# Transposing K on VectorE as 4-byte pairs, with scores in 32-row tiles and no row maximum, in a one-core attention kernel

## The chip, the cores and the metric

The kernel runs on one core of a Trainium2 chip. The metric is the device time of one execution in microseconds (us); less is better. Engines are called as in the profile: PE is TensorE (PEld its weight loads), DVE is VectorE, ACT is ScalarE, POOL is GpSimd, SP is SyncE, which issues the loads.

## The reference

Two independent attention blocks, A and B, run on their own inputs and their outputs are concatenated. Each block is:

```python
# x [16,64,640]  k_cache, v_cache [16,32,512,128]  wq [640,4096]  wo [4096,640], all bf16
q = (x @ wq).reshape(16, 64, 32, 128).transpose(0, 2, 1, 3)
scores = einsum("bhqd,bhkd->bhqk", q, k_cache) * 128 ** -0.5
p = softmax(scores, axis=-1)
o = einsum("bhqk,bhkd->bhqd", p, v_cache)
return o.transpose(0, 2, 1, 3).reshape(16, 64, 4096) @ wo
```

The caches are 16 x 32 x 512 x 128 x 2 bytes = 67 MB each, four of them, so about 268 MB of the 295 MB that are read are K and V. One property of the data matters for the experiments: x, K and wq are scaled so that a score has a standard deviation near 0.001. The softmax is therefore almost uniform, and the comparison with the reference cannot see keys that are taken in a wrong order. Where an experiment has a wrong key order on purpose, this is said, and its passing the comparison means nothing. For the same reason, where a version that moves the permutation is called right below, its key order rests on the indices of its access patterns, which lead to V's order; the comparison alone could not show it.

## The kernel before

The unit of work is two heads of two batches (a batch has 64 queries, so two batches fill 128 rows). Four engines run fixed orders of such units, shifted against each other like a pipeline; SP loads ahead into rings of buffers. For one unit PE transposes K (KX, 2 x 8 matmuls against the identity), DVE copies the result out of PSUM (KE), PE projects the queries (QP2), scores them (SM2), DVE takes row maxima (MX), ACT takes the exponential with the row sum (EX), DVE the reciprocal (RC2), POOL normalises (NM), PE transposes P (TR2), DVE copies it (TE2), then PE does PV and the output projection.

```python
PE_T = (("TR2", 1), ("QP2", 4), ("KX", 4, 0), ("SM2", 3), ("PV2", 1), ("XT", 0), ("OP2", 0), ("KX", 4, 1))
DVE_T = (("TE2", 1), ("RC2", 2), ("KE", 4, 0), ("MX", 3, 0), ("MX", 3, 1), ("KE", 4, 1), ("OVF", 0))
POOL_T = (("NM", 0, 0), ("NM", 0, 1))
# ... (cut)
def em_KX(e, op):                                    # PE: K to PSUM, transposed
    for t8 in range(8):
        ins = e.transpose(kt_ps[:, t8, :], kn_ring[:, c % NKB, j, hp, t8, :], ident[:, :])
def em_KE(e, op):                                    # DVE: PSUM to SBUF
    ins = e.tensor_copy(dst, src)                    # 128 x 1024 bf16
def em_SM2(e, op):                                   # PE: 4 matmuls, 128 rows x 64 columns
    ins = e.matmul(s_bank(sub)[64 * j:64 * j + 64, :], qT_ring[:, m % NQ, sub, 64 * j:64 * j + 64],
                   ktp_ring[:, m % NKT, sub, j, :], start=True, stop=True, tile_position=(0, 64 * j))
def em_MX(e, op):
    ins = e.reduce_max(negmax[:, r:r + 1], s_bank(g % 2), axis=AX.X, negate=True)
def em_EX(e, op):
    ins = e.activation(p_ring[:, g % NP, :], s_bank(g % 2), ACTF.Exp, bias=negmax[:, r:r + 1], scale=1.0,
                       accum_out=rowsum[:, r:r + 1])
def em_NM(e, op):                                    # POOL: normalise, and put keys in V's order
    src = p_ring[:, g % NP, :].rearrange("q (th tl pp) -> q th tl pp", th=2, tl=4)
    dst = pn_ring[:, g % NPN, :].rearrange("q (tl pp th) -> q th tl pp", tl=4, th=2)
    ins = e.tensor_scalar(dst, src, recip[:, r:r + 1], 1.0, ALU.mult, ALU.mult)
# ... (cut)
```

K and V are loaded in different key orders, so something has to permute the columns of P, and here POOL does it while it normalises. With `th=2`, consecutive elements of a run of `pp` are written two bf16 elements apart: a step of 4 bytes.

Of the kernel before, what the change touches and what calls it, by code (L numbers as in the profile page):

```python
# [6 lines left out]
F32 = mybir.dt.float32  # L7
ACTF = mybir.ActivationFunctionType
# [3 lines left out]
ENGINES = ("sp", "pe", "act", "dve", "pool")  # L12


class Cfg:
    G = 4
    HH = 16
    NKB = 5
    NVB = 5
    NX = 2  # L20
    NXN = 1
    XLEAD = 10
    NQ = 2
    NKT = 2
    NP = 4
    NPN = 3
    NT = 2
    NO = 2
    NR = 8
    PE_T = (("TR2", 1), ("QP2", 4), ("KX", 4, 0), ("SM2", 3), ("PV2", 1), ("XT", 0), ("OP2", 0), ("KX", 4, 1))  # L30
    ACT_T = (("QE2", 4), ("OE2", 1), ("XE", 0), ("EX", 3, 0), ("EX", 3, 1), ("OV", 0), ("ST", -1))
    DVE_T = (("TE2", 1), ("RC2", 2), ("KE", 4, 0), ("MX", 3, 0), ("MX", 3, 1), ("KE", 4, 1), ("OVF", 0))
    POOL_T = (("NM", 0, 0), ("NM", 0, 1))
    TAIL_SPLIT = 2
    SLOT_NS = 3600.0
    DMA_NS = dict(LDK=3100.0, LDV=3100.0, LDWQ=3900.0, LDWO=4300.0, LDX=700.0)


class Op:
    __slots__ = ("eng", "kind", "idx", "reads", "writes", "sem", "count", "deps", "waits", "dur", "ts", "aux",  # L40
                 "dma")

    def __init__(self, eng, kind, idx, reads=(), writes=(), dur=0.0, ts=None, aux=None):
        self.eng = eng
        self.kind = kind
        self.idx = idx
        self.reads = tuple(reads)
        self.writes = tuple(writes)
        self.sem = None
        self.count = None  # L50
        self.deps = []
        self.waits = []
        self.dur = dur
        self.ts = ts
        self.aux = aux
        self.dma = kind in ("LDK", "LDV", "LDX", "LDWQ", "LDWO", "ST")


STAGES = ("LDW", "LDX", "LDK", "LDV", "KX0", "KE0", "KX1", "KE1", "QP2", "QE2", "SM2", "MX0", "MX1", "EX0", "EX1",
          "RC2", "NM0", "NM1", "TR2", "TE2", "XT", "XE", "PV2", "OE2", "OP2", "OV", "ST")  # L60
STAGE_IDX = {s: i for i, s in enumerate(STAGES)}
SUB_KINDS = ("KX", "KE", "EX", "NM", "MX")


def build_plan(dims, cfg):
    NBLK, B, H = dims["NBLK"], dims["B"], dims["H"]
    G = cfg.G
    HH = min(cfg.HH, H)
    assert H % HH == 0 and HH % G == 0 and G % 2 == 0 and cfg.NR % 2 == 0 and B % 2 == 0
    NHALF = H // HH  # L70
    assert NHALF in (1, 2)
    NBP = B // 2
    SPB = HH
    NPASS = NBLK * NHALF
    NSTEP = NPASS * NBP * SPB
    NMAC = NSTEP // 2
    NCHUNK = NSTEP // G
    NGRP = NPASS * NBP
    HG = HH // G
    MPG = SPB // 2  # L80
    MPP = NBP * MPG
    MPC = G // 2
    KT = dims["KT"]

    def step_info(g):
        grp = g // SPB
        return grp // NBP, grp % NBP, grp, g % SPB

    progs = {e: [] for e in ENGINES}

    def mk(eng, kind, idx, reads, writes, stage, m_ts, sub=0, aux=None, dur=0.0):
        return Op(eng, kind, idx, reads, writes, dur=dur, aux=aux, ts=(m_ts, STAGE_IDX[stage], sub))

    OFF = {}
    for t in cfg.PE_T:
        OFF.setdefault(t[0], t[1])

    def make_op(kind, m, sub):
        g0, g1 = 2 * m, 2 * m + 1
        ps_, bp, grp, h0 = step_info(g0)  # L100
        c = g0 // G
        if kind == "KX":
            return mk("pe", "KX", (m, sub), [("kn", c % cfg.NKB, g0 % G), ("kn", c % cfg.NKB, g1 % G), ("ident",)],
                      [("KTB",)], "KX%d" % sub, m, sub)
        if kind == "KE":
            return mk("dve", "KE", (m, sub), [], [("KTB",), ("ktp", m % cfg.NKT, sub)], "KE%d" % sub, m, sub)
        if kind in ("MX", "EX", "NM"):
            g = 2 * m + sub
            r = g % cfg.NR
            if kind == "MX":  # L110
                return mk("dve", "MX", g, [], [("SB", sub), ("negmax", r)], "MX%d" % sub, m, sub)
            if kind == "EX":
                return mk("act", "EX", g, [("negmax", r)], [("SB", sub), ("p", g % cfg.NP), ("rowsum", r)],
                          "EX%d" % sub, m, sub)
            return mk("pool", "NM", g, [("p", g % cfg.NP), ("recip", r)], [("pn", g % cfg.NPN)], "NM%d" % sub, m, sub)
        r0, r1 = g0 % cfg.NR, g1 % cfg.NR
        if kind in ("XT", "XE"):
            mt = m + cfg.XLEAD
            if mt % MPG != 0 or not (0 <= mt < NMAC):
                return None  # L120
            gq = mt // MPG
            m_ts = mt - cfg.XLEAD + OFF["TR2"]
            if kind == "XT":
                return mk("pe", "XT", gq, [("xn", gq % cfg.NXN), ("ident",)], [("PTB",)], "XT", m_ts, aux=gq)
            return mk("act", "XE", gq, [], [("PTB",), ("xT", gq % cfg.NX)], "XE", m_ts, aux=gq)
        if kind == "QP2":
            return mk("pe", "QP2", m, [("xT", grp % cfg.NX), ("wq", ps_ % 2, h0 // G)], [("QB",)], "QP2", m)
        if kind == "QE2":
            return mk("act", "QE2", m, [], [("QB",), ("qT", m % cfg.NQ)], "QE2", m)
        if kind == "SM2":  # L130
            return mk("pe", "SM2", m, [("qT", m % cfg.NQ), ("ktp", m % cfg.NKT, 0), ("ktp", m % cfg.NKT, 1)],
                      [("SB", 0), ("SB", 1)], "SM2", m)
        if kind == "RC2":
            return mk("dve", "RC2", m, [("rowsum", r0), ("rowsum", r1)], [("recip", r0), ("recip", r1)], "RC2", m)
        if kind == "TR2":
            return mk("pe", "TR2", m, [("pn", g0 % cfg.NPN), ("pn", g1 % cfg.NPN), ("ident",)], [("PTB",)], "TR2", m)
        if kind == "TE2":
            return mk("dve", "TE2", m, [], [("PTB",), ("pT", m % cfg.NT)], "TE2", m)
        if kind == "PV2":
            return mk("pe", "PV2", m, [("pT", m % cfg.NT), ("v", c % cfg.NVB, g0 % G), ("v", c % cfg.NVB, g1 % G)],  # L140
                      [("OB",)], "PV2", m)
        if kind == "OE2":
            return mk("act", "OE2", m, [], [("OB",), ("oT", m % cfg.NO)], "OE2", m)
        if kind == "OP2":
            return mk("pe", "OP2", m, [("oT", m % cfg.NO), ("wo", ps_ % 2, h0 // G)], [("OUTB",)], "OP2", m)
        if kind in ("OV", "OVF", "ST"):
            if h0 + 1 != SPB - 1:
                return None
            last_half = ps_ % NHALF == NHALF - 1
            if kind == "OV":  # L150
                if NHALF == 1:
                    return mk("act", "OV", m, [], [("OUTB",), ("out_sb", grp % 2)], "OV", m, aux=grp)
                if last_half:
                    return None
                return mk("act", "OVP", m, [], [("OUTB",), ("outp", bp)], "OV", m, aux=grp)
            if kind == "OVF":
                if NHALF == 1 or not last_half:
                    return None
                return mk("dve", "OVF", m, [("outp", bp)], [("OUTB",), ("out_sb", grp % 2)], "OV", m, aux=grp)
            if NHALF == 1 or not last_half:  # L160
                return None
            return mk("act", "ST", m, [("out_sb", grp % 2)], [("out_dram", grp)], "ST", m, aux=grp)
        raise ValueError(kind)

    templates = {"pe": cfg.PE_T, "dve": cfg.DVE_T, "pool": cfg.POOL_T, "act": cfg.ACT_T}
    for eng, tmpl in templates.items():
        offs = [t[1] for t in tmpl] + [cfg.XLEAD]
        for k in range(-max(offs), NMAC - min(offs)):
            for t in tmpl:
                kind, off = t[0], t[1]  # L170
                sub = t[2] if len(t) > 2 else 0
                if kind in ("XT", "XE"):
                    op = make_op(kind, k, 0)
                    if op is not None:
                        progs[eng].append(op)
                    continue
                m = k + off
                if 0 <= m < NMAC:
                    op = make_op(kind, m, sub)
                    if op is not None:  # L180
# [7 lines left out]

    loads = []
    NEG = -10 ** 9  # L190
    for ps_ in range(NPASS):
        first_m = ps_ * MPP
        buf = ps_ % 2
        for j in range(HG):
# [68 lines left out]
    for eng in ENGINES:  # L263
        for op in progs[eng]:
            if not op.dma:
                assign(op)
# [453 lines left out]
```

## Time and profile before

| | before |
|---|---|
| median of 3 runs | 958.7 us (958.1 to 958.71) |
| busy share: PE / DVE / ACT / POOL | 96% / 88% / 59% / 44% |
| mean of one normalisation, K eviction, maximum, exponential | 843, 691, 681, 684 ns |
| read from HBM | 294.65 MB |

From the page of the kernel before: the busy time of each engine, then the span in 40 equal slices (a digit is the busy share in tenths; the last line is what the DMA engines moved in each slice).

```profile
PE 919.4 (96%) x14755; PEld 733.5 (77%) x15008; DVE 841.9 (88%) x1552; ACT 567.1 (59%) x1585; POOL 416.9 (44%) x518
...
PE   4999999999999999999999999999999999999997
...
POOL 0444444444444444444444444444444444444443
...
DMA  9999999999999999888999999988888988899830
GB/s 315 364 365 364 351 365 367 365 368 351 338 337 337 343 330 315 299 292 305 322 332 352 326 353 327 306 294 296 302 305 288 308 301 297 295 297 314 295 124 15
```

PE is full from the second slice on, at a granted clock of 0.998 on average. DMA moves about 365 GB/s while it fills the rings, and later follows PE, at 290 to 350.

From the same page, the chain of work that ended last (share of the span by engine), and four of its groups (line, engine, operation, output<-inputs, count | busy us, mean ns of one | idle before, and what ended it).

```profile
PE 89%; DVE 4%; POOL 3%; issue 2%; SPq 1%; DMA 1%; POOLq 0%; DVEq 0%
...
L496 POOL TENSOR_SCALAR pn_ring<-p_ring,recip 128x512 bf16<-128x512 bf16 x512 | 416.3, 843 | 532.7 <-DVE recip L488 532.7
L442 DVE COPY ktp_ring<-ps 128x1024 bf16<-128x1024 bf16 x512 | 353.7, 691 | 105.3 <-PE ps L433 85.1
L482 ACT ACTIVATE p_ring<-ps,negmax 128x512 bf16<-128x512 f32 x512 | 345.6, 684 | 4.8 <-DVE negmax L476 4.8
L476 DVE TENSOR_REDUCE negmax<-ps 128x1 f32<-128x512 f32 x512 | 327.3, 681 | 0.4 <-PE ps L467 0.3
```

So PE sets the pace. POOL's 843 ns per normalisation cost nothing here: it is idle for 532.7 us.

### The profile page before, as it was taken

What the parts mean: (1) busy time and instruction counts of PE and PEld (TensorE: products, weight loads), DVE (VectorE), ACT (ScalarE), POOL (GpSimd) and SP (SyncE); (2) the same over time, 40 slices, a digit from 0 to 9 for tenths busy, and PEclk for the clock granted to TensorE, in tenths of its full rate; (3) what the DMA queues carried; (4) which work ended last, traced back from release to release, by engine and by line L of the source; (5) the groups of instructions that cost most, each with busy time, mean ns of one, the idle gap of its engine ahead of it and who ended that gap; (6) DMA issues with size and microseconds to landing.
All of it is one profiled execution on the core that took longest, in us unless ns stands there. A gap on an engine that the chain in (4) does not pass through costs nothing.

```text
span 956.8 us, 34351 instructions
## 1 busy us (share of the span) xinstructions
PE 919.4 (96%) x14755; PEld 733.5 (77%) x15008; DVE 841.9 (88%) x1552; ACT 567.1 (59%) x1585; POOL 416.9 (44%) x518
## 2 busy tenths in 40 slices
PE   4999999999999999999999999999999999999997
PEld 3877777778777777877777787777877778777775
DVE  2898899898899999899999899889899998999996
ACT  1666656666665565656566666666666656565654
POOL 0444444444444444444444444444444444444443
PEclk9999999999999999999999999999999999999999
DMA  9999999999999999888999999988888988899830
GB/s 315 364 365 364 351 365 367 365 368 351 338 337 337 343 330 315 299 292 305 322 332 352 326 353 327 306 294 296 302 305 288 308 301 297 295 297 314 295 124 15
DMA packets 230871, 299.51 MB, mean 313 GB/s; under 512 B 9536, under 2 KB 165184, under 8 KB 230720
## 3 DMA queue, kind: packets, MB, share of 16 engines
q1 hardware_dynamic: 228416, 294.69, 91.0%
q8 instruction: 118, 1.93, 0.8%
q10 hardware_dynamic: 2304, 2.62, 0.8%
q14 instruction: 33, 0.27, 0.1%
HBM read 294.65 MB, written 2.62 MB: 311 GB/s over the span
## 4 chain that ended last, share of the span: by engine, by line
PE 89%; DVE 4%; POOL 3%; issue 2%; SPq 1%; DMA 1%; POOLq 0%; DVEq 0%
PE ps L433 22%; PE ps L524 14%; PE ps L451 14%; PE ps L467 14%; PE ps L505 12%; PE ps L545 7%; PE ps L540 5%; POOL pn_ring L496 3%; DVE out_sb L560 1%; DVE ktp_ring L442 1%; DVE pT_ring L512 1%; PE ps L604 1%; DMA xn_ring<-in_A_x_dram 1%; SPq L626 1%; SPq L583 1%
## 5 line engine op out<-in xcount | busy, mean ns | idle before, releaser
L496 POOL TENSOR_SCALAR pn_ring<-p_ring,recip 128x512 bf16<-128x512 bf16 x512 | 416.3, 843 | 532.7 <-DVE recip L488 532.7
L442 DVE COPY ktp_ring<-ps 128x1024 bf16<-128x1024 bf16 x512 | 353.7, 691 | 105.3 <-PE ps L433 85.1
L482 ACT ACTIVATE p_ring<-ps,negmax 128x512 bf16<-128x512 f32 x512 | 345.6, 684 | 4.8 <-DVE negmax L476 4.8
L476 DVE TENSOR_REDUCE negmax<-ps 128x1 f32<-128x512 f32 x512 | 327.3, 681 | 0.4 <-PE ps L467 0.3
L433 PE MATMUL ps<-ident,kn_ring 128*128 128x128 bf16 x4096 | 314.6, 220 | 2.8 <-DMA kn_ring<-in_A_k_cache_dram 1.6
L532 ACT ACTIVATE oT_ring<-ps 128x256 bf16<-128x256 f32 x256 | 98.0, 383 | 306.0 <-PE ps L524 306.0
L433 PEld LDWEIGHTS ps<-ident,kn_ring 128*128 128x128 bf16 x4096 | 251.9, 98 | 34.2 <-DVE ktp_ring L442 2.6
L524 PEld LDWEIGHTS ps<-pT_ring,v_ring 128*128 128x128 bf16 x4096 | 133.5, 98 | 109.2 <-issue 100.0
L451 PE MATMUL ps<-xT_ring,wq_sb 128*128 128x128 bf16 x2560 | 186.4, 220 | 3.2 <-DMA wq_sb<-in_A_wq_dram 3.2
L512 DVE COPY pT_ring<-ps 128x1024 bf16<-128x1024 bf16 x256 | 174.5, 682 | 4.6 <-PE ps L505 3.8
L524 PE MATMUL ps<-pT_ring,v_ring 128*128 128x64 bf16 x4096 | 163.8, 194 | 3.3 <-issue 1.7
L467 PE MATMUL ps<-ktp_ring,qT_ring 128*64 128x512 bf16 x1024 | 159.8, 392 | 0.4 <-ACT p_ring L482 0.4
L505 PE MATMUL ps<-ident,pn_ring 128*128 128x128 bf16 x2048 | 156.7, 219 | 3.5 <-POOL pn_ring L496 3.5
L451 PEld LDWEIGHTS ps<-xT_ring,wq_sb 128*128 128x128 bf16 x2560 | 155.2, 98 | 3.5 <-DMA wq_sb<-in_A_wq_dram 3.5
L459 ACT ACTIVATE qT_ring<-ps 128x256 bf16<-128x256 f32 x256 | 98.4, 384 | 66.8 <-PE ps L451 66.8
L505 PEld LDWEIGHTS ps<-ident,pn_ring 128*128 128x128 bf16 x2048 | 124.1, 98 | 7.0 <-POOL pn_ring L496 6.7
L545 PE MATMUL ps<-wo_sb,oT_ring 128*128 128x128 bf16 x512 | 112.1, 219 | 13.4
L482 ACT ACTIVATION_READ_ACCUMULATOR p_ring<-ps,negmax 128x1 f32 x512 | 105.0, 205 | 0.0
L540 PE MATMUL ps<-wo_sb,oT_ring 128*128 128x512 bf16 x259 | 97.8, 379 | 0.0
L540 PEld LDWEIGHTS ps<-wo_sb,oT_ring 128*128 128x128 bf16 x512 | 50.1, 98 | 30.6 <-ACT oT_ring L532 0.3
L467 PEld LDWEIGHTS ps<-ktp_ring,qT_ring 128*64 128x64 bf16 x1024 | 36.1, 108 | 27.1 <-ACT p_ring L482 0.6
L545 PEld LDWEIGHTS ps<-wo_sb,oT_ring 128*128 128x128 bf16 x512 | 50.1, 98 | 0.0
(13 smaller groups left out, 112.7 us busy)
## 6 DMA issues: line engine op xcount, KB each, us to landing
kn_ring<-in_A_k_cache_dram SPq DMA_DIRECT2D x128, 512.0 KB, 7.0
v_ring<-in_A_v_cache_dram SPq DMA_DIRECT2D x128, 512.0 KB, 7.2
kn_ring<-in_B_k_cache_dram SPq DMA_DIRECT2D x126, 512.0 KB, 4.8
v_ring<-in_B_v_cache_dram SPq DMA_DIRECT2D x126, 512.0 KB, 5.7
wq_sb<-in_A_wq_dram SPq DMA_DIRECT2D x8, 640.0 KB, 10.4
wo_sb<-in_A_wo_dram SPq DMA_DIRECT2D x8, 640.0 KB, 10.2
wq_sb<-in_B_wq_dram SPq DMA_DIRECT2D x8, 640.0 KB, 8.4
wo_sb<-in_B_wo_dram SPq DMA_DIRECT2D x8, 640.0 KB, 7.5
```

The source lines that it names most:

```text
L433: ins = e.transpose(kt_ps[:, t8, :], kn_ring[:, c % NKB, j, hp, t8, :], ident[:, :])
L442: ins = e.tensor_copy(dst, src)
L451: ins = e.matmul(q_ps[:, sub * 128:(sub + 1) * 128], wq_sb[:, ps_ % 2, kt, hh * DH:(hh + 1) * DH], xT_ring[:, grp % NX, kt, :], start=(kt ...
L467: ins = e.matmul(s_bank(sub)[64 * j:64 * j + 64, :], qT_ring[:, m % NQ, sub, 64 * j:64 * j + 64], ktp_ring[:, m % NKT, sub, j, :], start=T ...
L476: ins = e.reduce_max(negmax[:, r:r + 1], s_bank(g % 2), axis=AX.X, negate=True)
L482: ins = e.activation(p_ring[:, g % NP, :], s_bank(g % 2), ACTF.Exp, bias=negmax[:, r:r + 1], scale=1.0, accum_out=rowsum[:, r:r + 1])
L496: ins = e.tensor_scalar(dst, src, recip[:, r:r + 1], 1.0, ALU.mult, ALU.mult)
L505: ins = e.transpose(pt_ps[:, sub, t, :], pn_ring[:, g % NPN, t * 128:(t + 1) * 128], ident[:, :])
L512: ins = e.tensor_copy(pT_ring[:, m % NT].rearrange("p s t q -> p (s t q)"), pt_ps_flat)
L524: ins = e.matmul(o_ps[:, col:col + 64], v_ring[:, c % NVB, j, gi, t, :], pT_ring[:, m % NT, sub, t, 64 * j:64 * j + 64], start=(t == 0), s ...
L540: ins = e.matmul(out_ps0, oT_ring[:, m % NO, sub, :], wo_sb[:, ps_ % 2, hh, 0:N0], start=(hh == 0), stop=(hh == SPB - 1))
L545: last = e.matmul(out_ps1, oT_ring[:, m % NO, sub, :], wo_sb[:, ps_ % 2, hh, N0:DN], start=(hh == 0), stop=(hh == SPB - 1))
```

## The change

The intent is to take K's transposes off PE, the engine that is full. K is loaded with 16 keys per partition (4 KB rows instead of 2 KB). DVE transposes it with bf16 pairs taken as one 4-byte element, in blocks of 32x32 as the kernel's indices take them, which leaves the head dimension in a permuted order over 32 partitions. The columns of wq are permuted to match (POOL, once per chunk of four heads and block), and scores are summed over four rounds of eight 32-row tiles. The unit becomes a *pack* of four heads of two batches; there are 128 packs. The row maximum goes; at the end the row sums are checked, and if one lies outside 2^-40 to 2^40 a general second program with the maximum runs. Every operation gets its place in each engine's order from a table of times `AT`, in units of a pack.

```diff
-    PE_T = (("TR2", 1), ("QP2", 4), ("KX", 4, 0), ("SM2", 3), ...
-    DVE_T = (("TE2", 1), ("RC2", 2), ("KE", 4, 0), ("MX", 3, 0), ...
+    AT = dict(XT=-2 + 0.90, XE=-2 + 0.93, QP=-1 + 0.40, QE=-1 + 0.58, KT=(-1 + 0.08, -1 + 0.70), S=0.0,
+              EX=(0.20, 0.35, 0.55, 0.80), RC=(0.52, 0.93), NM=(0.54, 0.68, 0.95, 1.10),
+              TR=(0.95, 1.28), TE=(1.02, 1.38), PV=(1.20, 1.60), OE=(1.50, 1.72), OP=(1.70, 1.86),
+              OV=1.88, ST=1.885, WP0=-1.75, WP1=-6.0)
 ... (cut)
+    pending = sorted(loads, key=lambda e: (e[0], e[2]))
+    t_now = -8.0                                       # SP's order of loads is planned from here
 ... (cut)
-        def em_KX / em_KE                              # PE transposes, DVE evictions (cut)
+        def em_LDK(e, op):
+            src = blocks[blk][1][2 * bp + b, 4 * j:4 * j + 4].rearrange("h (p t) d -> (h p) (t d)", t=16)
+        def em_WP(e, op):                              # POOL: permute a chunk of wq, two copies (cut)
+        def em_KT(e, op):
+            dst = kt_ring[:, n % NKT, b].rearrange("p t j k two -> p (t j k two)").bitcast(F32)
+            ins = e.transpose(dst, kn_ring[:, n % NK, b, :].bitcast(F32))
+        def em_S(e, op):
+            for f in range(4):
+                for b in range(2):
+                    for i in range(4):
+                        rows = slice(32 * i, 32 * i + 32)
+                        last = e.matmul(ps[64 * b:64 * b + 64, i, :], qs_ring[rows, n % NQ, f, b, :],
+                                        kt_ring[rows, n % NKT, b, :, f // 2, :, f % 2],
+                                        start=(f == 0), stop=(f == 3), tile_position=(32 * i, 64 * b))
-            ins = e.activation(p_ring[...], s_bank(g % 2), ACTF.Exp, bias=negmax[:, r:r + 1], ...
+            ins = e.activation(p_ring[:, h % NP, :], ps[:, h % 4, :], ACTF.Exp, scale=1.0, ...
         def em_NM(e, op):
-            src = p_ring[:, g % NP, :].rearrange("q (th tl pp) -> q th tl pp", th=2, tl=4)
-            dst = pn_ring[:, g % NPN, :].rearrange("q (tl pp th) -> q th tl pp", tl=4, th=2)
+            src = p_ring[:, h % NP, :].rearrange("q (th tl k) -> q th tl k", th=4, tl=4)
+            dst = pn_ring[:, h % NPN, :].rearrange("q (tl k th) -> q th tl k", tl=4, th=4)
```

The last two lines follow from the new load. K now has 16 keys per partition while V still has 4, so the permutation has `th=4`: the normalisation writes runs of 32 elements with a step of 8 bytes instead of runs of 64 with a step of 4.

## The prediction

> **What bounds it now.** TensorE. The busy table has PE at 919 of 957 us, DVE 88%, ACT 59%, POOL 44%; the granted clock is full; 89% of the chain that ended last is PE. In the timeline one unit (two heads, two batches) is 3.56 us of PE work: K transposes 2x0.45, query projection 0.56, scores 0.55 plus 0.18 of switching, P transposes 0.45, PV 0.45, output 0.52. A pack of four heads is two units, 7.13 us; 128 packs are 913 us. DMA is second: in slices 1 to 9 its share is 0.9 or more at 365 GB/s, until the rings are full; later it follows at about 300 GB/s.
>
> **Per pack, what changes** (durations from the trace).
> - PE: the 32 K transposes go, -1.8 us. Scores become 32 matmuls in four rounds of eight 32x64 tiles. [...] this trace has two column tiles starting 4 ns apart and 240 ns per round of N=512. Four rounds plus two switches of 0.09 us: about 1.15 us, as now. PE: about 5.3 us.
> - DVE: K evictions (4x0.69) and maxima (4x0.64) go, 5.3 us. Added: two 128x1024 four-byte transposes and a 128x512 query eviction (0.66). No trace shows a DVE transpose[...]. DVE: 4.7 us instead of 6.9.
> - ACT loses the query evictions: 3.3 us. POOL keeps 4x0.84 = 3.4 us; in 16 packs it also permutes wq, about 4 us (estimate from 1.65 ns an element).
> - Order of work: reciprocal, two normalisations (1.63), P transposes (0.45), projection (1.12), its eviction (0.62), K transpose (1.15), next reciprocal, with latencies: about 5.5 us a pack. PE's own loop is also about 5.5.
>
> **DMA takes over.** Counting packets in 2 us slices of the saturated stretch, a 1 KB packet costs an engine 47 ns (347 GB/s over 16 engines), 1280 B 56 ns, 2 KB 86-87 ns. Extrapolated (estimate), the new 4 KB K packets cost about 165 ns, 397 GB/s. K then needs 338 us, V (unchanged, 1 KB) 386, wq 30, wo 29, x 7 (read once, not twice), out 7, instruction fetch about 8: **805 us**; 5.65 us per pack without weights. That is just above the 5.5 us of compute, so I expect DMA saturated nearly throughout: 805 + 2 to start + 9 from the last V to output and flag check + a few us of stalls at the block change, where POOL's permutation makes packs last 8 us.
>
> **Prediction: 822 us** (14% less); 8 in 10 between 797 and 862. Faster by over 2%: 0.97; within 2%: 0.02; slower: 0.01.
>
> **What would show the steps.** DMA share above 0.95 and 355-375 GB/s in nearly all slices; waits on landed loads (K for the DVE transpose, V for PV) instead of an unbroken PE chain; DVE transpose 1.15-1.25 us; a pack's score matmuls in 1.0-1.2 us; no general rerun.
>
> **What would make it wrong.** [...] Reading the score operand at a stride of 4 bytes, or wq at 8 bytes, slowing PE: up to 6.2 us a pack, 850 us. In-order waits that add up (one set of score banks, one PV bank): 6 us a pack, 830-850. The 4 KB packets at V's rate per byte: 850[...].

What is cut above, and marked, rested on no trace or run of this case. For PE, the cut sentence held that a round's eight tiles run beside each other; the trace of the kernel before shows this for two column tiles alone, 3 to 4 ns apart, so that PE's 5.3 us and the scores' 1.15 rest on an estimate of mine. For DVE, the cut sentence held the duration of one transpose, again an estimate of mine that no trace showed. "DVE: 4.7 us" came to that with about 2.4 us for the two transposes, and "K transpose (1.15)" in the order of work and the range 1.15 to 1.25 us further down are the same estimate.

## The result

| | before | after |
|---|---|---|
| median (lowest to highest) | 958.71 us (958.1 to 958.84), 4 runs | 948.87 us (948.03 to 952.19), 4 runs |
| ratio after / before, 95% interval | | 0.9903 (0.9885 to 0.9921): within 2% |
| busy share: PE / DVE / ACT / POOL | 96 / 88 / 59 / 44% | 78 / 61 / 44 / 74% |

A ratio here and below is the mean time of one kernel's runs over the mean of the other's of the same rounds on the same chip, so it is not quite the ratio of the medians that stand beside it.

The prediction was 822 us, 797 to 862. The kernel takes 127 us more than that. The work did leave PE (178 us of busy time) and DVE (264 us), and the time hardly moved: the question is where the gain went. From the page of the kernel after, the same lines as of before:

```profile
PE 741.5 (78%) x13905; PEld 524.2 (55%) x13905; DVE 577.9 (61%) x902; ACT 418.6 (44%) x1313; POOL 700.1 (74%) x550
...
PE   3077888888888888887677888888888888888884
...
POOL 2099777777777778788777878787878777777774
...
DMA  9999999989999998997579999999999999999820
GB/s 332 366 368 342 367 325 307 336 305 330 318 327 312 318 331 307 324 362 271 199 236 377 373 375 378 376 372 327 327 315 319 325 311 332 305 334 317 300 86 12
```

No engine is full. DMA is above 370 GB/s only in the stretch after the block change, where it refills rings; between the filling of the rings and the change, and again later, it follows something at 300 to 340. Its busy digits hide this, because they are 9 there too: from 100 to 400 us the share is 0.93 to 0.96 at 320 to 329 GB/s, while from 20 to 35 us, where the rings fill, it is 1.06 at 370 GB/s (records of packets overlap, so the share can pass 1). The rate tells more than the digit. Two steps of the prediction already fail here: DMA was to be saturated nearly throughout, and POOL, which was to stay near 3.4 us a pack, has 700.1 us instead of 416.9. The chain and the groups of the same page say more:

```profile
POOL 72%; DVE 11%; PE 10%; SPq 4%; issue 2%; DMA 1%; ACT 0%; ACTq 0%
POOL pn_ring L436 68%; DVE pT_ring L449 9%; PE ps L444 8%; POOL wqp_sb L357 2%; POOL wqp_sb L356 1%; SPq L349 1%; SPq L335 1%; DVE recip L429 1%; PE ps L380 1%; DMA ws_ring<-in_A_wq_dram 1%; SPq L342 1%; DVE kt_ring L393 1%; DVE qs_ring L386 0%; PE ps L403 0%; PE ps L460 0%
...
L436 POOL TENSOR_SCALAR pn_ring<-p_ring,recip 128x512 bf16<-128x512 bf16 x512 | 662.9, 1417 | 195.9 <-DVE recip L429 195.9
L416 ACT ACTIVATE p_ring<-ps 128x512 bf16<-128x512 f32 x512 | 304.0, 596 | 358.7 <-PE ps L403 358.7
...
L393 DVE STREAM_TRANSPOSE kt_ring<-kn_ring 128x1024 f32<-128x1024 f32 x256 | 315.9, 1234 | 7.5 <-DMA kn_ring<-in_A_k_cache_dram 7.5
```

The normalisation has the same shape and type as before, and takes 1417 ns instead of 843. It is 68% of the chain. POOL is not full all the same: it idles 195.9 us, waiting for reciprocals. The timeline shows how a normalisation that leaves POOL idle can nevertheless set the pace. This is one pack in the steady stretch of the kernel after (start us, duration us, engine, line, operation, [idle before <- what ended it]; rows of other work left out):

```profile
297.97 1.42 POOL L436 TENSOR_SCALAR pn_ring<-p_ring,recip 128x512 bf16<-128x512 bf16 x1
...
299.44 0.62 PE L444 MATMUL ps<-ident,pn_ring 128*128 128x128 bf16 x8 [0.25 <-POOL pn_ring L436]
...
299.77 0.20 ACT L416 ACTIVATION_READ_ACCUMULATOR p_ring<-ps 128x1 f32 x1
...
300.10 0.69 DVE L449 COPY pT_ring<-ps 128x1024 bf16<-128x1024 bf16 x1 [0.66 <-PE ps L444]
...
300.71 0.16 DVE L429 RECIPROCAL recip<-rowsum 128x2 f32<-128x2 f32 x1
300.96 5.17 POOL L436 TENSOR_SCALAR pn_ring<-p_ring,recip 128x512 bf16<-128x512 bf16 x4 [1.57 <-DVE recip L429]
...
302.98 0.12 DVE L429 RECIPROCAL recip<-rowsum 128x2 f32<-128x2 f32 x1
303.67 0.62 PE L444 MATMUL ps<-ident,pn_ring 128*128 128x128 bf16 x8 [0.83 <-POOL pn_ring L436]
```

Follow it down. The last normalisation of a pack ends at 299.39; only then can PE transpose that P (299.44); DVE evicts it (300.10); and the next pack's first reciprocal stands *behind* that eviction in DVE's order (300.71), although the second of its two row sums was there at 299.97 (the ACT row); only then can POOL start the next four normalisations (300.96). The second reciprocal comes at 302.98, in time, so the four run back to back in 5.17 us. A pack is 5.17 + 1.57 = 6.74 us, and measured from first reciprocal to first reciprocal, nearly every pack from the seventh on, outside the block change, is 6.72 to 6.75. The records of neighbouring normalisations overlap a little: four of 1.42 take 5.17.

The span adds up from such periods. The first reciprocal is at 15.5 us; 127 intervals at 6.73 are 855; the first eight intervals are 36 longer than that (the first alone 33, see the experiment on the head); the eight at the block change (9.11 to 10.13 each) are 23 longer; from the last pack's first reciprocal to the end are 16. Together 946, the span. A DMA-bound pack would need 5.65 by the prediction.

### The profile page after: what moved, and what is told of

It is laid out like the page before. It is cut to its first block, busy times and chain, and to the rows that moved or that the text cites. A ratio compares the mean times of both kernels' runs of the same rounds, so it can differ in the third digit from the quotient of the medians. Undisturbed runs are those within 1.5% of the kernel's fastest.

```text
span 946.3 us, 31604 instructions
## 1 busy us (share of the span) xinstructions
PE 741.5 (78%) x13905; PEld 524.2 (55%) x13905; DVE 577.9 (61%) x902; ACT 418.6 (44%) x1313; POOL 700.1 (74%) x550
## 4 chain that ended last, share of the span: by engine, by line
POOL 72%; DVE 11%; PE 10%; SPq 4%; issue 2%; DMA 1%; ACT 0%; ACTq 0%
POOL pn_ring L436 68%; DVE pT_ring L449 9%; PE ps L444 8%; POOL wqp_sb L357 2%; POOL wqp_sb L356 1%; SPq L349 1%; SPq L335 1%; DVE recip L429 1%; PE ps L380 1%; DMA ws_ring<-in_A_wq_dram 1%; SPq L342 1%; DVE kt_ring L393 1%; DVE qs_ring L386 0%; PE ps L403 0%; PE ps L460 0%
## 5 line engine op out<-in xcount | busy, mean ns | idle before, releaser
L436 POOL TENSOR_SCALAR pn_ring<-p_ring,recip 128x512 bf16<-128x512 bf16 x512 | 662.9, 1417 | 195.9 <-DVE recip L429 195.9
L416 ACT ACTIVATE p_ring<-ps 128x512 bf16<-128x512 f32 x512 | 304.0, 596 | 358.7 <-PE ps L403 358.7
L393 DVE STREAM_TRANSPOSE kt_ring<-kn_ring 128x1024 f32<-128x1024 f32 x256 | 315.9, 1234 | 7.5 <-DMA kn_ring<-in_A_k_cache_dram 7.5
L444 PE MATMUL ps<-ident,pn_ring 128*128 128x128 bf16 x2048 | 159.9, 221 | 184.6 <-POOL pn_ring L436 184.6
L380 PE MATMUL ps<-xT_ring,wqp_sb 128*128 128x128 bf16 x2560 | 170.9, 224 | 2.1 <-POOL wqp_sb L357 1.3
L474 PE MATMUL ps<-wo_sb,oT_ring 128*128 128x512 bf16 x512 | 167.6, 385 | 0.0
L380 PEld LDWEIGHTS ps<-xT_ring,wqp_sb 128*128 128x128 bf16 x2560 | 156.8, 115 | 3.3 <-ACT p_ring L416 1.7
L403 PE MATMUL ps<-kt_ring,qs_ring 32*64 32x512 bf16 x4096 | 146.9, 398 | 1.9 <-DVE kt_ring L393 1.9
L386 DVE TENSOR_SCALAR qs_ring<-ps 128x512 bf16<-128x512 f32 x128 | 88.5, 692 | 52.6 <-PE ps L380 52.6
L416 ACT ACTIVATION_READ_ACCUMULATOR p_ring<-ps 128x1 f32 x512 | 105.4, 206 | 0.0
L403 PEld LDWEIGHTS ps<-kt_ring,qs_ring 32*64 32x64 bf16 x4096 | 55.5, 104 | 41.6 <-DVE kt_ring L393 2.2
```

Of the source, the lines that this page charges most:

```text
L380: last = e.matmul(ps[:, 0, f * 128:(f + 1) * 128], w[:, kt, f, :], xT_ring[:, xs, kt, :], start=(kt == 0), stop=(kt == KT - 1))
L386: ins = e.tensor_scalar(qs_ring[:, op.idx % NQ].rearrange("p f b q -> p (f b q)"), ps[:, 0, :], scale, None, ALU.mult)
L393: ins = e.transpose(dst, kn_ring[:, n % NK, b, :].bitcast(F32))
L403: last = e.matmul(ps[64 * b:64 * b + 64, i, :], qs_ring[rows, n % NQ, f, b, :], kt_ring[rows, n % NKT, b, :, f // 2, :, f % 2], start=(f = ...
L416: ins = e.activation(p_ring[:, h % NP, :], ps[:, h % 4, :], ACTF.Exp, scale=1.0, accum_out=rowsum[:, h:h + 1])
L436: ins = e.tensor_scalar(dst, src, recip[:, (h // 2) % NR, h % 2:h % 2 + 1], 1.0, ALU.mult, ALU.mult)
```

## The experiments

The theory: the 8-byte destination step makes the normalisation 1.7 times as long, and this length, through the hand-over above (the 1.57 us between a pack's last normalisation and the next pack's first), sets the pace; with the step back at 4 bytes, DMA takes over as predicted. The rivals: POOL is slowed by the DVE transposes that now run beside it; it is the shorter runs (32 instead of 64), not the step; or the time went to the start and the block change. The last two experiments keep the long normalisation and ask which order of work sets the 6.73 us of a pack.

### e1_step4B: the destination step alone, back at 4 bytes

```diff
-            src = ... "q (th tl k) -> q th tl k", th=4, tl=4      dst = ... "q (tl k th) -> q th tl k", tl=4, th=4
+            src = ... "q (th tl pp) -> q th tl pp", th=2, tl=4    dst = ... "q (tl pp th) -> q th tl pp", tl=4, th=2
```

The key order is wrong: everything else is the kernel after.

> Only the normalisation's destination changes: step 4 bytes in runs of 64, as the kernel before has it (wrong values on purpose, the same amount of work). Theory (the 8-byte step of POOL's writes makes the normalisation slow): 1417 ns falls to about 843 ns, the steady pack from 6.73 us to 5.65-5.8 us (DMA or the rest of the chain), the time to about 825 us (119 steady packs times 1.0 us less; the start and the block change keep most of their loss). Rival A (POOL is slowed by VectorE's new SBUF-to-SBUF transposes): the normalisation stays above 1.3 us and the time at 949. Rival B (in-order waits other than POOL set the pack): the normalisation falls to 0.84 us but the pack stays above 6.3 us, time above 900.

Measured: 828.5 us (826.16 to 831.45), ratio to before 0.8643 (0.8617 to 0.867). Its page, the normalisation and the DMA lines, and POOL's timeline in the same stretch:

```profile
DMA  9999999999999999999989999999999999999980
GB/s 329 364 372 369 378 377 376 378 374 377 374 375 376 361 378 377 379 371 371 330 285 376 375 377 377 374 376 376 380 369 377 376 374 378 375 373 375 378 286 13
...
L436 POOL TENSOR_SCALAR pn_ring<-p_ring,recip 128x512 bf16<-128x512 bf16 x512 | 418.3, 846 | 317.8 <-DVE recip L429 317.8
```

```profile
298.61 1.62 POOL L436 TENSOR_SCALAR pn_ring<-p_ring,recip 128x512 bf16<-128x512 bf16 x2 [1.57 <-DVE recip L429]
300.85 1.65 POOL L436 TENSOR_SCALAR pn_ring<-p_ring,recip 128x512 bf16<-128x512 bf16 x2 [0.62 <-DVE recip L429]
```

One access pattern is worth 120 us. The normalisation is back at 846 ns, DMA is saturated in nearly all slices, and outside the start and the block change nearly all packs are 5.45 to 6.9 us, about 5.9 on average, as loads allow. The hand-over of 1.57 us is still there; but with it POOL's round is about 4.8 us (3.27 + 1.57), shorter than the 5.45 that PE needs, so it no longer sets anything.

### e5_step4B_run32: step 4 bytes, runs of 32

```diff
-            src = ... "q (th tl k) -> q th tl k"            dst = ... "q (tl k th) -> q th tl k"
+            src = ... "q (two a k) -> q two a k", k=32      dst = ... "q (a k two) -> q two a k", k=32
```

Wrong key order; runs are as short as in the kernel after.

> The normalisation writes runs of 32 elements, as the kernel after does, but at a 4-byte step (wrong values on purpose). Theory (the step decides, not the length of the runs): 0.83-0.87 us each, time about 828 us. Rival (short runs cost POOL a restart each): above 1.1 us.

Measured: one run, 829.25 us, state unknown; the normalisation takes 844 ns in its profile. So it is the step, not the length of the runs; this rests on the duration in one profile.

### e3_before_8B: the kernel before with the 8-byte step

```diff
-            src = ... th=2, tl=4        dst = ... "q (tl pp th) -> q th tl pp", tl=4, th=2
+            src = ... th=4, tl=4        dst = ... "q (tl k th) -> q th tl k", tl=4, th=4
```

There is no DVE transpose in this kernel, and the step is all that it has of the change. Wrong key order.

> The kernel before with the kernel after's 8-byte step in the normalisation (wrong values on purpose); no DVE transpose in it. Theory: the normalisation goes from 843 to about 1417 ns although nothing else changed; POOL has 3.56 us per unit for 2.83, so the time stays within 2% (958-980). Rival A: the normalisation stays at 0.84 us, time 958.

Measured: 1118.34 us (1118.08 to 1118.86), ratio 1.1666 (1.1646 to 1.1685). Its chain and its normalisation:

```profile
POOL 57%; DVE 18%; PE 18%; issue 4%; SPq 1%; DMA 1%; POOLq 0%; DVEq 0%
...
L496 POOL TENSOR_SCALAR pn_ring<-p_ring,recip 128x512 bf16<-128x512 bf16 x512 | 679.7, 1411 | 427.3 <-DVE recip L488 427.3
```

The normalisation takes 1411 ns without any DVE transpose: contention with the transposes is refuted as its cause. The size of the result was a surprise: the expectation was a kernel that stays near PE's pace, since POOL's work of 2 x 1.33 us fits in a unit of 3.56. It does not fit in the *loop*, as a line of POOL's timeline in this run shows:

```profile
306.18 2.65 POOL L496 TENSOR_SCALAR pn_ring<-p_ring,recip 128x512 bf16<-128x512 bf16 x2 [1.57 <-DVE recip L488]
```

Two normalisations take 2.65, then P is transposed and evicted, and the next reciprocal stands behind that eviction in DVE's order: again 1.57 us of hand-over. A unit takes 2.65 + 1.57 = 4.22 us, with POOL 61% busy. The kernel before has the same hand-over in its order, and hides it only because its normalisations are short.

### e2_exp_permutes: the permutation moved to ACT

```diff
-            ins = e.activation(p_ring[:, h % NP, :], ps[:, h % 4, :], ACTF.Exp, ...
+            dst = p_ring[:, h % NP, :].rearrange("q (tl k th) -> q th tl k", tl=4, th=4)
+            ins = e.activation(dst, <ps, h % 4, as "q th tl k">, ACTF.Exp, ...
     em_NM: src and dst contiguous
```

The result is right.

> Right result: ScalarE's exp writes the permuted order (8-byte step), POOL's normalisation is contiguous on both sides. Theory: the normalisation takes at most 843 ns; if ScalarE does not mind the step, exp stays at 0.60 us, pack 5.65-5.8 us, time about 825 us. If ScalarE minds it as POOL does, exp goes to about 1.0 us, ScalarE to about 5 us a pack and the chain scores-exp-projection grows by 0.4-1.6 us: 6-7 us a pack, 860-950 us. Rival A: the normalisation stays above 1.3 us.

Measured: 925.1 us (923.0 to 926.64), ratio 0.9645 (0.9625 to 0.9666). The exponential with the 8-byte step and the contiguous normalisation:

```profile
ACT 56%; PE 33%; POOL 4%; SPq 4%; issue 2%; DMA 1%; DVE 0%; ACTq 0%
...
L418 ACT ACTIVATE p_ring<-ps 128x512 bf16<-128x512 f32 x512 | 660.0, 1343 | 185.3 <-PE ps L403 185.3
L439 POOL TENSOR_SCALAR pn_ring<-p_ring,recip 128x512 bf16<-128x512 bf16 x512 | 349.3, 696 | 481.4 <-DVE recip L432 481.3
```

ACT pays the same way: 1343 ns against 596 contiguous. The chain moves from POOL to ACT and a pack takes 6.62 us. The step's cost is no peculiarity of POOL.

### e7_kt_8B: half of the permutation in DVE's transpose

The DVE transpose writes 4-byte elements. Let it write one bit of the key order with a step of 8 bytes; the normalisation keeps the other bit, a step of 4 bytes. The result is right.

```diff
-        kt_ring = sb("kt_ring", [128, NKT, 2, 16, 2, 32, 2], BF16)
+        kt_ring = sb("kt_ring", [128, NKT, 2, 8, 2, 32, 2, 2], BF16)
-            ins = e.transpose(dst, kn_ring[:, n % NK, b, :].bitcast(F32))
+            dst = flat.rearrange("p (aj k h) -> p h aj k", k=32, h=2)
+            src = kn_ring[:, n % NK, b, :].bitcast(F32).rearrange("p (h aj r) -> p h aj r", h=2, r=32)
+            ins = e.transpose(dst, src)
     em_S reads kt_ring with the one more dimension; em_NM: "q (two c) -> q two c" to "q (c two) -> q two c"
```

> Right result. Half of the permutation moves into the DVE transpose of K, whose four-byte destination elements now step by 8 bytes; the normalisation writes at a 4-byte step. If VectorE does not mind its step, the transpose stays at 1.23 us, the normalisation is 0.85 us and the time 825-832 us as in the run with the 4-byte step. If VectorE minds as POOL and ScalarE did (about double), the transpose is 2.2 us, VectorE 6.7 us a pack and the time 880-920 us.

Measured: 828.3 us (827.74 to 828.76), ratio 0.8637 (0.8622 to 0.8651); the normalisation takes 848 ns. From its page, the transpose:

```profile
L395 DVE STREAM_TRANSPOSE kt_ring<-kn_ring 128x1024 f32<-128x1024 f32 x256 | 316.3, 1236 | 7.3 <-DMA kn_ring<-in_A_k_cache_dram 7.2
```

1236 ns against 1234 contiguous: an 8-byte step of 4-byte elements costs DVE nothing, where an 8-byte step of 2-byte elements more than doubles the time of POOL's and ACT's operations (1417 ns against 692 to 696, 1343 against 596). This is a kernel with the right result that has all of what the wrong-order version had.

### e8_kt_16B: all of the permutation in DVE's transpose

```diff
     as e7_kt_8B, with h=4: the transpose writes with a step of 16 bytes; em_NM: src and dst contiguous
```

The result is right.

> Right result. The whole permutation moves into the DVE transpose (16-byte step of four-byte elements); the normalisation is contiguous, 0.70 us as where exp permuted. If VectorE does not mind: transpose 1.23 us, time 820-830 us, bound by DMA as with the 4-byte step, so hardly better than it. If it minds: transpose 2.2 us or more, 880-920 us.

Measured: 856.13 us (855.43 to 857.28), ratio 0.8928 (0.8913 to 0.8943); the normalisation takes 692 ns. From its page:

```profile
PE 48%; DVE 38%; SPq 4%; POOL 4%; issue 3%; DMA 2%; ACT 0%; ACTq 0%
...
L395 DVE STREAM_TRANSPOSE kt_ring<-kn_ring 128x1024 f32<-128x1024 f32 x256 | 519.6, 2030 | 7.3 <-DMA kn_ring<-in_A_k_cache_dram 7.3
```

At 16 bytes DVE pays too, 2030 ns. The time lies between the two outcomes that were expected: a pack is 6.05 us, and DVE is 86% busy and in the chain.

### e14_exp_4B: the permutation split between ACT and POOL

```diff
     em_EX: dst = ... "q (c two) -> q two c", two=2 (step 4 bytes); em_NM as in e7_kt_8B (step 4 bytes)
```

The result is right.

> Right result: exp writes at a 4-byte step and the normalisation writes at a 4-byte step, each doing half of the permutation. The normalisation is 0.85 us. If ScalarE at 4 bytes costs as little extra as POOL does (a fifth), exp is 0.6-0.75 us and the time 826-832, bound by DMA; if it pays in proportion to its 8-byte case, exp is about 0.97 us, the loop scores-exp-projection grows by 0.4 us or more, 840-880 us.

Measured: 827.74 us (827.31 to 830.28), ratio 0.8642 (0.8625 to 0.866); the exponential takes 757 ns and the normalisation 847. Two 4-byte steps cost far less than one of 8: 161 and 151 ns more than contiguous writes (596 and 696), against 747 on ACT and 721 on POOL for one of 8. The pace is DMA's again, so this version and the one with the split transpose take the same time.

### e4_head: loads planned from later on

The second thing in the after trace is the first interval of 40 us instead of 6.7. POOL's timeline of the kernel after shows it:

```profile
10.50 1.26 POOL L357 COPY wqp_sb<-ws_ring 128x1280 bf16<-128x1280 bf16 x1
45.00 1.26 POOL L356 COPY wqp_sb<-ws_ring 128x1280 bf16<-128x1280 bf16 x1 [33.24 <-DMA ws_ring<-in_A_wq_dram]
46.20 1.26 POOL L357 COPY wqp_sb<-ws_ring 128x1280 bf16<-128x1280 bf16 x1
47.43 5.12 POOL L436 TENSOR_SCALAR pn_ring<-p_ring,recip 128x512 bf16<-128x512 bf16 x4
```

POOL waits 33.24 us for the third chunk of wq, and the first normalisations stand behind it in POOL's order. That chunk needs a free slot of its two-slot ring; the plan of SP's order starts eight packs early, so it fills the rings of K and V first, and SP issues the third chunk only at 35.5 us. DMA was not idle: from 20 to 35 us it moved 370 GB/s.

```diff
-    t_now = -8.0
+    t_now = -2.2
```

The result is right.

> Only the order of the loads at the start changes (the planner's start 5.8 slots later puts the third to eighth wq loads among the first K and V loads). Theory (POOL's in-order queue holds the first normalisations behind the third wq permutation, whose load comes at 45 us): the first normalisation starts at 17-20 us instead of 47, the steady pack stays 6.73 us, time 915-922 us. Rival (the start is bound by the amount of data to load): the time stays within 5 us of 949.

Measured: 928.02 us (924.89 to 930.63), ratio 0.9683 (0.9653 to 0.9713). The first interval falls from 40 to 8.1 us, the steady packs stay at 6.72 to 6.74. It gives 21 us, not the whole 33, because the next four packs are 8.5 to 10.6 us and the four after them 7.1 to 7.4; that is a little less than was expected. The start explains 2% of the time, not the missing 13%.

### e9_kt8_head and e9b_kt8_head: the late plan, where DMA sets the pace

```diff
     e7_kt_8B with t_now = -2.2 (e9b_kt8_head is the same kernel again, as the partner of the next experiment)
```

> The previous right version with the 4-byte step, plus the other order of loads at the start. Theory (with the normalisation repaired the kernel is bound by DMA, and DMA is busy through the stalled start anyway): 0-10 us less than without the order, 815-830 us. Rival (the stalled start costs its full 21 us, as it did where POOL set the pace): 803-810 us.

> The same kernel as the last right version, again, as the partner of the run with the moved wq permutation on the same chip: 822-827 us.

Measured: 824.49 us (822.0 to 826.12), ratio 0.8589 (0.8568 to 0.8611), and, again, 825.75 us, ratio 0.8607 (0.8591 to 0.8623). The same edit that gave 21 us gives about 4 here (3 by the ratio of the repeat), though it removes the same stall. Where DMA is the limit, the bytes that were loaded during the stall do not have to be loaded later, so the engines' idle start costs little.

### e10_kt8_head_wp: wq's permutation later, at the block change

```diff
     e9_kt8_head, and:
-              OV=1.88, ST=1.885, WP0=-1.75, WP1=-6.0)
+              OV=1.88, ST=1.885, WP0=-1.75, WP1=-5.15)
```

At -6.0 the permutation of a chunk (2.5 us) lies between the third and the fourth normalisation of a pack in POOL's order, where it holds up the second pair's transposes. The edit puts it between the pairs, where POOL waited 0.62 us for a reciprocal in any case. The result is right.

> Right result: the 4-byte step, the other order of loads at the start, and POOL's second set of wq permutations moved from between the last two normalisations of a pack to behind the first two. Theory: at the block change a pack lasts under 7.5 us instead of 7.84-8.9, which DMA, busy with the weights, partly hides: 816-824 us, at most 8 us less than without. If the change does not cost at all: 824.

Measured: 822.12 us (821.39 to 823.11), ratio 0.8571 (0.8559 to 0.8583), against 0.8607 of its partner. The DMA lines and the chain of its page:

```profile
DMA  9999999999999999999999999999999999999980
GB/s 322 370 371 371 380 377 377 376 373 379 370 380 375 370 376 374 375 376 354 370 370 375 372 377 370 372 378 375 378 375 375 377 367 380 375 372 376 380 281 13
...
PE 65%; SPq 13%; DMA 12%; issue 4%; POOL 4%; DVE 2%; ACT 0%; ACTq 0%
```

The first seven packs of the change fall to 7.15 us (7.83 to 8.25 in the partner), and DMA keeps at least 354 GB/s through it. The first eight packs together are 8 us shorter than the partner's, but the next eight are 6 us longer, so most of what the edit gained there was given back; between the medians of the two kernels 3.6 us remain. This is the fastest version with a right result, and it beats both kernels.

### e11_kt8_halfV: fewer bytes

```diff
     e7_kt_8B, and from the sixth pack on V is loaded for two of the four heads only
```

The result is wrong (relative error 0.94).

> The right version with the 4-byte step, but from the sixth pack on only half of V is loaded (wrong values on purpose): DMA has a quarter less to move, every engine the same work. Theory (DMA sets 828 us, the engines' own chain is 5.46 us a pack): all steady packs 5.45-5.5 us, DMA share about 0.75, time 775-795 us (111 packs of 5.46, and the same start, block change and end). Rival (the engines set it): 820-830 us.

Measured: 789.96 us (788.87 to 791.04), ratio 0.8241 (0.8229 to 0.8254). Nothing but the bytes changed, and 38 us went (ratio 0.8637 to 0.8241). Away from the start and the change, nearly all packs are now 5.45 to 5.56 us, and PE is busy without a gap, as one stretch of `--windows` shows (us; busy us of PE, PEld, DVE, ACT, POOL; granted clock, DMA share, GB/s):

```profile
100.00:200.00 100.00, 99.95 (x1984) 72.95 (x1982) 82.17 (x130) 59.18 (x188) 60.20 (x74) 1.00 0.91 302
```

So the 828 us of the versions with the 4-byte step are set by DMA, and the engines' own loop is 5.46 us, PE's.

### e12_order: the second P transposes later in the order

If the hand-over is what adds 1.57 us to POOL's round, the order can remove it: let the eviction that stands ahead of the reciprocal come later.

```diff
-              TR=(0.95, 1.28), TE=(1.02, 1.38), PV=(1.20, 1.60), ...
+              TR=(0.95, 1.45), TE=(1.02, 1.56), PV=(1.20, 1.62), ...
```

The result is right; the 8-byte step stays.

> The kernel after with its 8-byte step, right result; only the static order changes: TensorE projects the next queries before it transposes the second half of P, and VectorE evicts that transpose behind the reciprocal. Theory (the pack is a loop through the orders: reciprocal, two normalisations, P transposes, projection, its eviction, K transpose, reciprocal): the projection leaves the loop, pack about 6.1 us (5.9-6.4), time 870-905. Rival (POOL is simply full at 5.3 us of normalisation plus hand-over): the pack stays at 6.7 us, time 945-950.

Measured: 951.29 us (950.26 to 952.7), ratio 0.9916 (0.9901 to 0.9932). The expectation failed: nothing was gained. POOL did leave the chain, and another loop of 6.78 us took over, as the chain of its page shows:

```profile
PE 64%; ACT 9%; DVE 9%; POOL 8%; SPq 4%; issue 4%; DMA 1%; ACTq 0%
```

Reading the steps of that chain in time: scores, exponential, query projection, P transposes, their eviction, PV, output, the other P transposes, next scores. PE waits for one thing after the other in its fixed order, and the order was what was edited. So the edit traded one loop for another, and by itself says little about the hand-over.

### e13_rc_order: only the reciprocal earlier

The same question with an edit that does not touch PE's order: DVE takes a pack's first reciprocal before the previous pack's last eviction.

```diff
-              RC=(0.52, 0.93)
+              RC=(0.37, 0.93)
```

The result is right; the 8-byte step stays.

> The kernel after with its 8-byte step, right result; VectorE computes a pack's first reciprocal before it evicts the last pack's second P transpose, not behind it. Theory (the loop is: four normalisations 5.17 us, then 1.57 us of hand-over through P transpose, its eviction and the reciprocal behind it in VectorE's order): the hand-over falls away and the next loop binds (two normalisations, P transposes, scores, two exps, reciprocal: 2.6 plus 3.5 us), pack 6.0-6.2 us, time 860-885. Rival (the pack of 6.73 us is set elsewhere, as the failed reordering could mean): 6.6 us or more, 935-950.

Measured: 924.25 us (922.21 to 925.36), ratio 0.9644 (0.9628 to 0.9661): faster, less than was expected. Its chain, and POOL's timeline:

```profile
POOL 41%; PE 25%; DVE 25%; SPq 4%; issue 3%; DMA 1%; ACT 0%; ACTq 0%
```

```profile
301.27 2.67 POOL L436 TENSOR_SCALAR pn_ring<-p_ring,recip 128x512 bf16<-128x512 bf16 x2 [0.38 <-DVE recip L429]
304.34 2.69 POOL L436 TENSOR_SCALAR pn_ring<-p_ring,recip 128x512 bf16<-128x512 bf16 x2 [0.40 <-DVE recip L429]
```

The wait of 1.57 us is gone: 0.38 to 0.75 is left before each run of normalisations. A pack is 6.48 us all the same, and the chain now alternates POOL, PE and DVE. In time, one round of it is (each term counted up to where the next one starts, as records overlap): two normalisations 2.67, P transposes 0.46, projection 1.31, its eviction 0.61, K transpose 1.16, reciprocal 0.15, with 0.12 of latencies: 6.48. That is the "order of work" of the prediction, term by term, with 2.67 where it had 1.63 for the two normalisations: 5.5 + 1.04 = 6.54.

So the kernel after has two loops of nearly the same length, 6.73 (POOL's round and the hand-over) and 6.48 (the prediction's order of work). The long normalisation is in both, four times in the first and twice in the second. Removing the hand-over exposes the second; only shortening the normalisation removes both, which is what the version with the 4-byte step showed.

## Why the prediction was wrong

The step that failed stands in two places of the prediction: "POOL keeps 4x0.84 = 3.4 us", and "two normalisations (1.63)" in the order of work. I took the duration of the old normalisation for the new one because shape, type and engine are the same. The diff changes its destination step from 4 to 8 bytes, as two lines of it show, and I did not cost that. Measured: 1417 ns each and 5.17 us a pack. I worried in the prediction about the strides of what PE *reads* (the scores took 1.14 us a pack, as predicted; a weight load of wq took 115 ns on average, 98 before) and not about the step of what POOL *writes*.

| step of the prediction | predicted | measured | |
|---|---|---|---|
| PE per pack | 5.3 us, own loop about 5.5 | 5.46 (with fewer bytes) | right |
| scores, 32 tiles | about 1.15 us | 1.14 | right |
| DVE transpose 128x1024 | 1.15 to 1.25 us, an estimate | 1.234 | right |
| POOL per pack | 3.4 us | 5.17 | **wrong: the step** |
| order of work | 5.5 us | 6.48 once exposed; 6.73 set the pace | wrong by the same term |
| wq permutation on POOL | about 4 us a chunk | 2.5 | too high |
| 4 KB packet | 165 ns | 164 ns (median record, kernel after, 500 to 620 us, saturated) | right |
| DMA takes over | nearly throughout, 355 to 375 GB/s | only with the 4-byte step: 369 to 380 in most slices | followed from the wrong term |
| block change | a few us | 23 us | too small |
| start | 2 us | 33 us of POOL idle; worth 21 us here, 4 where DMA sets the pace | missed |
| general rerun | none | none | right |

Two of the right rows rested on what no trace of the kernel before showed. The trace of the kernel after shows both. Score tiles of 32 rows run beside each other: in the pack at 304.22 us the tiles of the first round start 3 to 4 ns apart, those of later rounds up to 15, and the 32 score matmuls in four rounds take 1.14 us. The DVE transpose of 128x1024 elements of 4 bytes takes 1234 ns.

Where did the gain go, then? Not to DMA, whose mean rate stayed where it was (313 GB/s before, 314 after), and not to contention: the normalisation takes 1411 ns without a DVE transpose in the kernel. PE's saved 178 us became waits for POOL's results (the transposes of P waited 184.6 us for the normalisation). With the step alone at 4 bytes the kernel takes 828.5 us, inside the predicted range; with the start and the change mended as well, and a right result, 822.1. The agreement of that last number with the predicted 822 is partly luck: the prediction counted neither the stall at the start nor the repair of it.

The prediction also had no step for an engine that is not full and yet sets the pace. It named in-order waits that add up as a risk, but for the score and PV banks, and at 6 us a pack. It added up one order of work and compared it with busy times; the hand-over loop (last normalisation, transpose, eviction, reciprocal behind it, first normalisation) was not in it. At 0.84 us a normalisation that loop is about 4.8 us and can be left out, at 1.42 it is 6.73 and cannot.

What stays open: why the 8-byte step of 2-byte writes costs so much. The runs show when it costs, on which engines and how much, and no counter that would show the mechanism. The block change's 23 us was only partly taken apart: moving the permutation of wq helped where DMA set the pace, but no run moved it in the kernel with the 8-byte step. And that a pack of 6.48 us is the next limit behind 6.73 is shown by one reordering; no run removed both loops and kept the 8-byte step.

## What to carry to other kernels

When a change touches the layout of an operand, compare the byte step of every access pattern in every operation that reads or writes it, also in operations that seem unchanged and on engines that have time to spare; a duration from the old trace holds only for the old pattern (here 843 ns at a step of 4 bytes and 1417 at 8, with the same shape and type). Walk each in-order loop across engines, not only busy shares: POOL set the pace of two kernels here at 61% and 74% busy, because what it delivered came back to it through the queues of two other engines. If a permutation has to be written, split it, or put it where the elements are wide: a 4-byte step of bf16 (843 to 848 ns on POOL against 692 to 696 contiguous, 757 against 596 on ACT), or an 8-byte step of 4-byte elements (1236 ns on DVE against 1234), was cheap or free here, and one 8-byte step of bf16 (1411 to 1425 ns on POOL, 1343 on ACT) was not.

## Durations by step and by packet, as measured here

- **The step of the destination on POOL.** The normalisation, a bf16 write of 128x512, took 692 to 696 ns contiguous, 843 to 848 at a step of 4 bytes, and 1411 to 1425 at a step of 8 bytes.
- **The step of the destination on ACT.** The exponential of 128x512 from PSUM to bf16 took 596 ns contiguous, 757 at 4 bytes, 1343 at 8 bytes.
- **The step in elements.** A step of 4 bf16 elements doubles POOL's and ACT's time (1417 ns against 692 to 696, 1343 against 596), and a step of 2 costs 147 to 161 ns in 512 elements. DVE's 4-byte writes are free at a step of 2 elements (1236 against 1234 ns) but not at 4 (2030 ns).
- **The DVE transpose of 4-byte elements.** 128x1024 took 1234 ns with contiguous writes, 1236 with an 8-byte step, and 2030 with a 16-byte step.
- **What a packet takes by its size, on loads issued by SP.** In a saturated stretch of the kernel after (500 to 620 us, 371 to 380 GB/s) the median record of a 1 KB packet is 48 ns, of 1280 bytes 59, and of 4 KB 164 ns; the records overlap there (share of the 16 engines 1.06 to 1.07).
